# One three-level store instead of two half stores for a batch's last 64 output rows

## The chip, the cores and the metric

One core of one Trainium2 chip runs the kernel. The metric is the device time of one execution in microseconds (us); lower is better. It is quoted as the median of 3 runs. Beside it stands one profiled execution, with its own time, its span (from the first to the last instruction of the program) and its trace.

## The reference

Three stages follow each other on 4 batches of 576 rows: an attention over 8 heads with two sparse masks, a mixture of 4 causal attention experts with a top-2 gate, and a gated convolution block. All is float32 at the interface. Cut to what matters here, the last stage is:

```
x  = sparse_attention(q, k, v)            # [4, 576, 512]
x  = mixture_of_experts(x, ...)           # [4, 576, 512]
h  = max(x @ w_in, 0)                     # [4, 576, 1024]
c  = conv over 3 rows of h, one weight per channel
out = (h * sigmoid(c)) @ w_out            # [4, 576, 512]
```

The store of `out` is what changes. A batch has 576 = 4 x 128 + 64 output rows of 512 floats.

## The kernel before, in words

Every part of the work is a Python generator (a unit) of a kind: L loads, S the sparse attention, W weights, V, Q and A the experts' attention, M the gate of the last block, N its output product. A long string `ORDER` names, two characters at a time, which unit takes its next step. That string is the order in which each engine gets its instructions. It is the same before and after.

The units that matter here are `m_out` (batches 0 to 2, one unit per output tile) and `m_last` (batch 3, all five tiles in one unit). Both end in `m_put`, which copies an output tile from PSUM to an SBUF tile `ob` on ScalarE (ACT, through the helper at line 139) and then stores it with a DMA issued by SyncE (SP). `ob` has two buffers, which are used in turn.

Tiles t = 0 to 3 are 128 rows of 512 floats and are stored by one DMA at L733. Tile t = 4 has only 64 rows. Its product is computed in two halves of 256 columns, side by side in the partitions (L707): columns 0 to 255 of the 64 rows stand in partitions 0 to 63, and columns 256 to 511 of the same rows in partitions 64 to 127. In the output the two halves of a row lie next to each other. Line 736 stores them with two DMAs, one for each half.

SP issues all loads and stores of this kernel but the loads of `w_out`, and the 80 DMA transposes of the attention weights (L629, from `pn` to `apt`), in one queue and in the order of `ORDER`. Each DMA takes the next of eight completion semaphores (DMAHW0 to DMAHW7) and waits for the DMA that used it eight DMAs earlier. At the end of the program (L939) SP waits for every one of these semaphores, and the engines meet at a barrier.

Of the kernel before, what the change touches and what calls it, by code (L numbers as in the profile page):

```python
# [95 lines left out]
def moe_stack_kernel(ctx, tc, qk_in, vloc, vstr, w_p, wo_t, w_in, conv_w, w_out, out):  # L96
    nc = tc.nc
    ctx.enter_context(tc.manual_schedule())
    B, S, _ = vstr.shape
# [38 lines left out]
    def copy_a(out, in_, scale=1.0):  # L138
        act.activation(out=out, in_=in_, func=ACTF.Copy, scale=scale)  # L139
# [547 lines left out]
    def m_out(b, t):  # L687
        ps = bank("o")
        q0 = 128 * t
        half = DM // 2  # L690
        ps = ps if t < NG else ps[:, 0:half]
        for f in range(KF):
            g = [x[:, f % 2, q0:min(q0 + 128, S)] for x in gT[b, f - f % 2]]
            m_mul(ps, t, g, f)
            if f % 2:
                yield
        yield from m_put(b, t, ps)
# [13 lines left out]
    def m_last(b):  # L711
        for k in range(KF // 2):
            if k == 0:
                pairs = [banks("oe") for _ in range(2)]
                ends.extend([p[:, n] for p in pairs for n in range(2)] + [bank("o")[:, 0:DM // 2]])
            for t in range(NT):
                q0 = 128 * t
                for f in (2 * k, 2 * k + 1):
                    m_mul(ends[t], t, [x[:, f % 2, q0:min(q0 + 128, S)] for x in gT[b, 2 * k]], f)
                yield  # L720
        for t in range(NT):
            yield from m_put(b, t, ends[t])
            if t < NT - 1:
                yield

    def m_put(b, t, ps):
        q0 = 128 * t
        half = DM // 2
        ob = late["g"].tile([128, DM], F32, tag="ob", bufs=2, name="ob")
        copy_a(ob[:, 0:ps.shape[1]], ps, 1.0 / (G_S * W_S))  # L730
        yield
        if t < NG:
            nc.sync.dma_start(out=out[b, q0:q0 + 128, :], in_=ob)  # L733
        else:
            for n in range(2):
                nc.sync.dma_start(out=out[b, q0:S, half * n:half * n + half], in_=ob[64 * n:64 * n + 64, 0:half])


    late = {"pf": pool("pf", PF_BUFS), "pt": pool("pt", PF_BUFS), "z": pool("z", Z_BUFS),
# [204 lines left out]
```

## Time and profile before

| what | value |
|---|---|
| median of 3 runs | 378.42 us (377.3 to 379.41) |
| the profiled execution | 378.94 us |
| its span | 377.2 us |
| TensorE (PE) busy | 341.3 us, 90% |
| mean granted TensorE clock | 0.986 of full speed |
| stores of 128 x 512 (L733) | 16 DMAs of 256 KB |
| half stores of 64 x 256 (L736) | 8 DMAs of 64 KB, two for each batch |

The span is 1.7 us shorter than the profiled execution's time; the rest lies around it. Of the four pairs of half stores, three are issued while other work goes on (from 213.6, 313.2 and 334.7 us) and one, from 373.4 us, is the last thing that the program does.

### The profile page before, as it was taken

What the parts mean: (1) busy time and instruction counts of PE and PEld (TensorE: products, weight loads), DVE (VectorE), ACT (ScalarE), POOL (GpSimd) and SP (SyncE); (2) the same over time, 40 slices, a digit from 0 to 9 for tenths busy, and PEclk for the clock granted to TensorE, in tenths of its full rate; (3) what the DMA queues carried; (4) which work ended last, traced back from release to release, by engine and by line L of the source; (5) the groups of instructions that cost most, each with busy time, mean ns of one, the idle gap of its engine ahead of it and who ended that gap; (6) DMA issues with size and microseconds to landing.
All of it is one profiled execution on the core that took longest, in us unless ns stands there. A gap on an engine that the chain in (4) does not pass through costs nothing.

```text
span 377.2 us, 12596 instructions
## 1 busy us (share of the span) xinstructions
PE 341.3 (90%) x5139; PEld 227.8 (60%) x5139; DVE 309.0 (82%) x729; ACT 278.8 (74%) x628; POOL 59.4 (16%) x194
## 2 busy tenths in 40 slices
PE   4167699999789999999999999999999999999995
PEld 3146466667557666777557577776555576564542
DVE  6889879999969999999988758999998858693520
ACT  2468657878878998988887589997895796753522
POOL 8533430111400003000031005001000030000000
PEclk9999989999969999999999999999999999999999
DMA  7997968555867971893025724244536574010003
GB/s 269 285 271 221 285 221 235 164 167 124 119 86 122 181 123 30 195 162 69 3 58 127 121 58 106 47 79 85 100 76 120 79 134 90 20 53 28 3 26 127
DMA packets 79210, 45.94 MB, mean 122 GB/s; under 512 B 63792, under 2 KB 72496, under 8 KB 79152
## 3 DMA queue, kind: packets, MB, share of 16 engines
q1 hardware_dynamic: 78000, 40.94, 50.3%
q0 software_dynamic: 1152, 4.19, 3.5%
q8 instruction: 40, 0.66, 0.7%
q14 instruction: 18, 0.15, 0.1%
HBM read 25.20 MB, written 4.72 MB: 79 GB/s over the span
## 4 chain that ended last, share of the span: by engine, by line
PE 52%; ACT 17%; DVE 13%; DMA 13%; issue 4%; SPq 1%; POOL 0%; ACTq 0%; POOLq 0%; DVEq 0%
PE o L704 14%; DMA apt<-pn 7%; PE oe L704 6%; PE zav L638 4%; PE hps L145 4%; PE hps L146 3%; PE hps L147 3%; ACT pn L139 3%; PE o L707 2%; DMA vn<-in_dram 2%; PE psq L145 2%; DMA st<-in_dram 2%; PE psq L146 2%; PE psq L147 2%; ACT apf L602 2%
## 5 line engine op out<-in xcount | busy, mean ns | idle before, releaser
L704 PE MATMUL o<-wout,hs 128*128 128x512 f16 x288 | 66.2, 379 | 0.0
L704 PEld LDWEIGHTS <-hs 128*128 128x128 f16 x384 | 36.6, 98 | 41.9 <-issue 1.6
L673 DVE SCALAR_TENSOR_TENSOR t<-hs,taps,t 128x576 f32<-128x576 f32 x64 | 48.7, 809 | 6.4 <-ACT t L139 6.4
L139 ACT ACTIVATE pn<-apf,aden 64x64 f16<-64x64 f32 (+4 forms) x80 | 42.4, 557 | 9.2 <-DVE aden L611 2.8
L625 DVE SCALAR_TENSOR_TENSOR pn<-apf,aden,pn 128x320 f16<-128x320 f32 (+4 forms) x80 | 42.2, 544 | 6.1 <-ACT pn L139 5.4
L145 PE MATMUL psq<-xt,wqk 128*128 128x288 f16 x128 | 37.9, 296 | 1.0 <-DVE anm L593 0.7
L145 PE MATMUL hps<-z,wp 128*128 128x288 f16 x128 | 36.7, 287 | 1.6 <-ACT hs L665 1.0
L146 PE MATMUL psq<-xt,wqk 128*128 128x288 f16 x128 | 37.7, 295 | 0.0
L147 PE MATMUL psq<-xt,wqk 128*128 128x288 f16 x128 | 37.7, 295 | 0.0
L147 PE MATMUL hps<-z,wp 128*128 128x288 f16 x128 | 36.6, 286 | 0.0
L146 PE MATMUL hps<-z,wp 128*128 128x288 f16 x128 | 36.6, 286 | 0.0
L602 ACT ACTIVATE apf<-asc,anm 64x64 f32<-64x64 f32 (+3 forms) x64 | 29.7, 468 | 5.3 <-DVE anm L587 3.5
L620 POOL MEMSET pn<- 128x64 uint32 (+1 forms) x80 | 10.8, 153 | 130.6 <-DMA apt<-pn 80.0
L638 PE MATMUL zav<-apt,v 128*64 128x128 f16 (+1 forms) x720 | 27.4, 220 | 3.4 <-DMA apt<-pn 2.0
L638 PEld LDWEIGHTS <-v 128*64 128x64 f16 x720 | 22.1, 110 | 11.9 <-issue 10.9
L665 ACT ACTIVATE hs<-hps 128x576 f32<-128x576 f32 x32 | 20.6, 648 | 11.1 <-PE hps L147 6.4
L679 DVE SCALAR_TENSOR_TENSOR t<-t,hs 128x1152 f32<-128x1152 f32 x16 | 21.4, 1351 | 6.5 <-ACT t L677 6.5
L677 ACT ACTIVATE t<-t 128x1152 f32<-128x1152 f32 x16 | 18.6, 1162 | 9.1 <-DVE t L673 9.1
L136 POOL COPY bn<-lp 32x320 f32<-32x320 f32 x31 | 16.8, 543 | 51.7 <-PE av L377 32.5
L586 DVE TENSOR_REDUCE anm<-asc 64x2 f32<-64x128 f32 (+3 forms) x32 | 21.6, 674 | 2.7 <-PE asc L578 2.7
L139 ACT ACTIVATE t<-hs,taps 128x576 f32<-128x576 f32 x32 | 23.5, 770 | 0.1
L139 ACT ACTIVATE qk<-psq 128x576 f16<-128x576 f32 x32 | 20.3, 647 | 2.9 <-PE psq L147 2.0
(183 smaller groups left out, 812.3 us busy)
## 6 DMA issues: line engine op xcount, KB each, us to landing
st<-in_dram SPq DMA_DIRECT2D x9, 512.0 KB
ow<-in_dram POOLq DMA_DIRECT2D x8, 512.0 KB, 9.4
out_dram<-ob SPq DMA_DIRECT2D x16, 256.0 KB
ul<-in_dram SPq DMA_DIRECT2D x12, 288.0 KB
ul<-in_dram SPq DMA_DIRECT2D x12, 252.0 KB
vs<-in_dram SPq DMA_DIRECT2D x16, 144.0 KB
vn<-in_dram SPq DMA_DIRECT2D x8, 256.0 KB
st<-in_dram SPq DMA_DIRECT2D x4, 386.0 KB
```

The lines of the kernel that those rows point to most:

```text
L139: act.activation(out=out, in_=in_, func=ACTF.Copy, scale=scale)
L145: nc.tensor.matmul(out=out, lhsT=ah, rhs=bh, start=first, stop=False)
L146: nc.tensor.matmul(out=out, lhsT=al, rhs=bh, start=False, stop=False)
L147: nc.tensor.matmul(out=out, lhsT=ah, rhs=bl, start=False, stop=last)
L586: dve.tensor_reduce(out=nm[:, 0], in_=asc[:rows, :, :w], axis=mybir.AxisListType.X, op=ALU.max)
L602: act.activation(out=pfs[par], in_=scs[par], func=ACTF.Exp, scale=C2, bias=nm[:, 0, par:par + 1], accum_out=den[:, par:par + 1])
L625: dve.scalar_tensor_tensor(out=pn[:, 1, :w], in0=pfs[par], scalar=den[:, par:par + 1], in1=pn[:, 0, :w], op0=ALU.mult, op1=ALU.subtract)
L638: nc.tensor.matmul(out=av[64 * par:64 * par + 64, 0:rows], lhsT=v2[a][:, kb, D * e:D * e + D], rhs=pts[par][:, l, kb], start=(kb == 0 and ...
L665: act.activation(out=hs[:, i, 1:S + 1].rearrange("p (a n) -> p a n", a=2), in_=ps, func=ACTF.Relu, scale=1.0 / W_S)
L673: dve.scalar_tensor_tensor(out=t_[:, i], in0=tap, scalar=w, in1=t_[:, i], op0=ALU.mult, op1=ALU.add)
L679: dve.scalar_tensor_tensor(out=t_, in0=t_, scalar=1.0, in1=hs[:, :, 1:S + 1], op0=ALU.add, op1=ALU.mult)
L704: nc.tensor.matmul(out=ps, lhsT=g[a], rhs=wout[l][:, f], **at)
```

## The change

The two DMAs become one. Its DRAM side is written as a pattern of three levels: 2 halves, 64 rows, 256 floats. Its SBUF side is the whole tile: 128 partitions of 256 floats. The bytes and where they land are the same.

```
         else:
-            for n in range(2):
-                nc.sync.dma_start(out=out[b, q0:S, half * n:half * n + half], in_=ob[64 * n:64 * n + 64, 0:half])
+            nc.sync.dma_start(out=out[b, q0:S].rearrange("p (n c) -> n p c", n=2), in_=ob[:, 0:half])
```

On the other engines the instructions and their order are unchanged. On SP one instruction goes in each batch. Before, in SP's queue, around batch 0's last tile (`apt<-pn` is a transpose, `out_dram<-ob` a store, the shape is that of the DMA's destination):

```order
L629 DMA_TRANSPOSE apt<-pn_176 128x2x64 [waits DVE_49,DMAHW1_49,PE_49,Pool_49]
L736 DMA out_dram<-ob 64x256
L736 DMA out_dram<-ob 64x256 [waits DMAHW7_49]
L629 DMA_TRANSPOSE apt<-pn_174 128x2x64 [waits DVE_49,DMAHW0_49,PE_49,DMAHW2_49,Activation_49,Pool_49]
L629 DMA_TRANSPOSE apt<-pn_175 128x2x64 [waits DMAHW3_49,PE_49]
```

And after, in the same place:

```order
L629 DMA_TRANSPOSE apt<-pn_176 128x2x64 [waits DVE_49,DMAHW1_49,PE_49,Pool_49]
L735 DMA out_dram<-ob 2x64x256
L629 DMA_TRANSPOSE apt<-pn_174 128x2x64 [waits DVE_49,DMAHW2_49,PE_49,DMAHW7_49,Activation_49,Pool_49]
L629 DMA_TRANSPOSE apt<-pn_175 128x2x64 [waits DMAHW3_49,DMAHW0_49,PE_49]
```

One store stands where two stood, and each later DMA takes a semaphore that is one lower in the round. The end of SP's queue before, with the last stores of batch 3:

```order
L733 DMA out_dram<-ob 128x512 [waits DMAHW6_49,Activation_49]
L733 DMA out_dram<-ob 128x512 [waits DMAHW7_49,Activation_49]
L736 DMA out_dram<-ob 64x256 [waits DMAHW0_49,Activation_49]
L736 DMA out_dram<-ob 64x256 [waits DMAHW1_49]
L939 UNCONDITIONAL_BRANCH
```

And after:

```order
L733 DMA out_dram<-ob 128x512 [waits DMAHW3_49,Activation_49]
L733 DMA out_dram<-ob 128x512 [waits DMAHW4_49,Activation_49]
L735 DMA out_dram<-ob 2x64x256 [waits DMAHW5_49,Activation_49]
L938 UNCONDITIONAL_BRANCH
```

The last store was the one on DMAHW1, and is now on DMAHW5, four DMAs having gone in all.

## Rows read from the trace of the kernel before

**Rows 1.** The profile's page: span, and the chain that ended last, by engine.

```profile
span 377.2 us, 12596 instructions
...
PE 52%; ACT 17%; DVE 13%; DMA 13%; issue 4%; SPq 1%; POOL 0%; ACTq 0%; POOLq 0%; DVEq 0%
```

**Rows 2.** Chain of waits, 366 to 378 us: start, length, what.

```profile
368.22 3.88 PE o L704 x18
372.11 0.80 PE o L707 x12
372.90 0.03 ACTq L139
372.93 0.04 issue
372.98 0.39 ACT ob L139
```

**Rows 3.** Timeline of SP's queue, 364 to 378 us: start, length, what.

```profile
366.29 6.86 SPq L733 DMA_DIRECT2D out_dram<-ob  x5
373.39 1.12 SPq L736 DMA_DIRECT2D out_dram<-ob  x2
```

**Rows 4.** Stores' issues on SP: ns min/median/max, first and last start.

```profile
L733 SPq DMA_DIRECT2D out_dram<-ob x16: 332/342/585, 193.8 to 372.8; - x16
L736 SPq DMA_DIRECT2D out_dram<-ob x8: 472/588/591, 213.6 to 373.9; - x8
```

**Rows 5.** Stretches of the end: engines' busy time, PE clock, DMA share, GB/s.

```profile
373.70:374.10 0.40, 0.00 (x0) 0.00 (x0) 0.00 (x0) 0.00 (x0) 0.00 (x0) 1.00 1.01 394
374.50:375.10 0.60, 0.00 (x0) 0.00 (x0) 0.00 (x0) 0.00 (x0) 0.00 (x0) 1.00 0.45 109
375.10:375.70 0.60, 0.00 (x0) 0.00 (x0) 0.00 (x0) 0.00 (x0) 0.00 (x0) 1.00 0.44 109
375.70:376.00 0.30, 0.00 (x0) 0.00 (x0) 0.00 (x0) 0.00 (x0) 0.00 (x0) 1.00 0.00 0
```

**Rows 6.** SP's own L939 instructions, 375.95 to 376.5 us; SP's waits from 374.

```profile
L939 SPq EVENT_SEMAPHORE  x7: 28/28/28, 376.0 to 376.4; - x7
L939 SPq DRAIN  x2: 7/7/7, 376.4 to 376.5; - x2
...
SPq L939 <- DMA out_dram<-ob: 1.3, 2, 0.8
```

**Rows 7.** Loads of 18 x 8 x 256 (L321): SP's timeline, then stretches as in rows 5.

```profile
93.70 0.88 SPq L321 DMA_DIRECT2D vs<-in_dram  x2
...
168.41 3.65 SPq L321 DMA_DIRECT2D vs<-in_dram  x3
...
95.40:95.60 0.20, 0.20 (x12) 0.20 (x6) 0.20 (x2) 0.20 (x1) 0.20 (x1) 1.00 0.51 179
95.60:95.80 0.20, 0.20 (x12) 0.16 (x8) 0.17 (x2) 0.20 (x1) 0.20 (x1) 1.00 0.53 189
172.20:172.40 0.20, 0.20 (x4) 0.17 (x2) 0.20 (x2) 0.20 (x1) 0.00 (x0) 1.00 0.57 205
```

**Rows 8.** SP's timeline around the half stores of batches 0, 1 and 2.

```profile
213.61 1.22 SPq L736 DMA_DIRECT2D out_dram<-ob  x2
215.94 8.62 SPq L629 DMA_TRANSPOSE apt<-pn  x5
...
313.18 1.22 SPq L736 DMA_DIRECT2D out_dram<-ob  x2
328.76 2.35 SPq L733 DMA_DIRECT2D out_dram<-ob  x2
334.66 1.11 SPq L736 DMA_DIRECT2D out_dram<-ob  x2
345.63 0.34 SPq L733 DMA_DIRECT2D out_dram<-ob  x1
```

**Rows 9.** Batch 0: two stretches as in rows 5, then the timelines of POOL, ACT, DVE.

```profile
214.70:216.00 1.30, 0.47 (x16) 0.50 (x17) 0.96 (x6) 0.68 (x4) 0.16 (x1) 1.00 0.41 101
216.90:217.50 0.60, 0.60 (x7) 0.48 (x6) 0.60 (x3) 0.60 (x4) 0.00 (x0) 1.00 0.24 55
...
218.33 0.15 POOL L620 MEMSET pn<- 128x64 uint32 x1 [3.40 <-DMA apt<-pn]
...
218.85 0.45 ACT L139 ACTIVATE pn<-apf,aden 128x192 f16<-128x192 f32 x1
...
219.41 0.42 DVE L625 SCALAR_TENSOR_TENSOR pn<-apf,aden,pn 128x192 f16<-128x192 f32 x1 [0.72 <-ACT pn L139]
...
221.39 1.19 SPq L629 DMA_TRANSPOSE apt<-pn  x1
```

## The prediction

> **What bounds the kernel now.** I began with the page. Over the whole span the chain that ended last is half TensorE, and the DMA part of it is 13% [rows 1]; but a change of one store can only matter where a store is waited for, so the page's averages say little here. Next I read the chain's last pieces. The reader is to see that TensorE's last product ends at about 372.9 us and ACT's last copy at 373.4 us [rows 2]. That leaves 377.2 - 373.4 = 3.8 us in which no engine computes. Then I read SP's timeline for the same stretch: the last pair of half stores is issued from 373.39 to 374.51 [rows 3]. What follows is bound by DMA alone, and the stretches show it: the first half's data moves between 374.5 and 375.1, the second's between 375.1 and 375.7, at 109 GB/s in each (109 x 0.6 = 65 KB, one half of 64 KB), and after 375.7 nothing moves [rows 5]. SP sees the last landing at 376.0, and the waits for the other queues, the drain and the barrier take the rest [rows 6].
>
> So this end has a price that counts in full, about 2.2 us from the first byte to the last landing's being seen and 0.7 of issue, while the other three pairs lie in the middle of the kernel, where they count only if someone waits for them.
>
> **The change part by part.**
>
> *The issue.* One issue goes. The half stores take 472 to 591 ns each on SP [rows 4], so 0.6 us of SP's time is saved per batch. In the last batch the second half's data could not start before its own issue; in the other three SP's next instruction starts later anyway: at 215.94 after an end at 214.83, at 328.76 after 314.40, at 345.63 after 335.77 [rows 8]. I take nothing for those three. In the new store the first byte moves where the first half's moved before, at 374.5, 1.1 us after the issue began at 373.39; if its issue is one of the long ones (591 against 472), 0.1 later.
>
> *How many DMA engines carry it.* This is the term that decides. 128 packets of 1 KB have to move in either case. If all 16 engines share them, that is 8 each. The trace has a transfer that shows how the sharing goes: the loads of L321 write 18 x 8 x 256 floats, 144 packets of 1 KB, which 16 engines could share as 9 each. Where two or three such loads are queued and little else moves, the DMA share is 0.51 to 0.57 [rows 7], while a store of 128 rows reaches 1.01 [rows 5]. 9 of 16 engines is 0.56, and 9 is the largest divisor of 18 that is not over 16. So these engines are dealt by the outermost count of the pattern and not by the number of packets. The new store's DRAM side begins with a count of 2; its SBUF side with 128. If the smaller decides, 2 engines move 64 packets each. No transfer in this trace has sides that begin with different counts, so I bound the term from both sides: 16 engines as for the 128-row stores, or 2. The value I take is 2, because the outermost count is what the nearest row follows and a split into more than 2 would have to cut inside the DRAM side's first level.
>
> The Trainium skill, "DMA: Bandwidth & Descriptors", in "Why a DMA increments its semaphore by 16 and not by 1", says that the number of engines is the largest number up to 16 that divides the slowest dimension of both sides; by it 18 rows give 9, as the trace has it, and the new store 2, which is the forecast below. The same page, in "Rules for kernel authors", advises against two transfers to disjoint partition halves and for one transfer of 128 partitions; by that sentence alone the change would gain, which is the first rival.
>
> *The price of a packet.* In the two stretches of the loads 189 and 205 GB/s over 9 engines are 21.0 and 22.8 GB/s each, or 49 and 45 ns for 1024 bytes [rows 7]. The half stores themselves are dearer: 0.45 x 16 x 0.6 us / 64 = 67 ns for a packet [rows 5]; but there 16 engines read 64 partitions at once. The 128-row store moves 394 / (1.01 x 16) = 24.4 GB/s per engine, 42 ns for each KB [rows 5]. Two engines alone should not crowd each other, so I take 48 ns, the middle of the loads' two figures and a little, and keep 42 and 67 as the ends: 64 x 48 = 3.1 us, from 2.7 to 4.3.
>
> *The sum at the end.* Data moved from 374.5 to 375.65, 1.1 us (the stretch to 375.7 holds all of it). Now it takes 3.1 us from the same start: +2.0. Against that, SP's final waits. After the last landing it still had seven semaphore waits and a drain to go through, from 376.0 to 376.4 [rows 6], 0.06 us each. The last store was on DMAHW1 and is now on DMAHW5. If SP goes through the queues by number, four of these waits are done before the landing: -0.24 (an estimate from that row, as the row does not name the queues). Landing, barrier and ACT's copy before are as they were. Sum: +1.75 us, 378.94 + 1.75 = 380.7 for an execution like the profiled one, with 1.7 us around the span. The profiled execution is 0.5 above the median of the runs, so the forecast for the median is 378.42 + 1.75 = 380.2 us.
>
> *The stores in the middle.* The store of batch 0 would keep two engines until 214.7 + 3.1 = 217.8, where both halves were done by 216.0 [rows 9]. SP issues the next transposes from 215.94, and their data moves in 216.9 to 217.5 [rows 9]; on two engines it would queue behind the store, so that the first transpose lands 0.4 to 0.9 us later. Behind it wait POOL's memset at 218.33, which had waited 3.40 us for a transpose, and ACT's copy to the same `pn` at 218.85; after them DVE's step at 219.41, and only at 221.39 the transpose that uses it [rows 9]. Between DVE's end at 219.83 and that transpose lie 1.5 us. I cost this at nothing; what hides it is TensorE's work, for which this transpose waits in any case. With 67 ns packets the store would hold the engines to 219.0, the first transpose would be 1.5 to 2 us late, ACT's queue would stand still, and up to 0.7 could come through. After batches 1 and 2 SP issues nothing for 14 and 10 us, so a store of 3 to 4 us delays nobody.
>
> **The rivals.**
>
> *All 16 engines (faster).* The new transfer is dealt by the SBUF side's 128 partitions. For it: every 128-row store is, and both halves were. Against it: rows 7. Then 128 x 67 / 16 = 0.54 us of data from 374.5, ending at 375.1 instead of 375.65, and -0.24: -0.8 us, 377.6.
>
> *Two engines with dear packets, and a delay that comes through (slower beyond 0.5%).* Place: the last store, and the transposes behind batch 0's. Price: 64 x 67 = 4.3 us, +3.2 - 0.24 = +2.9 at the end, and 0 to 0.7 at batch 0: 381.4 to 382.0. It decides from 51 ns per packet on, where the end alone passes +1.9. For it: the only 1 KB stores in this trace take 67. Against it: these had 16 engines on 64 partitions, and the 2 KB stores take 42 per KB with all engines busy.
>
> *Hidden anyway.* If the end of the program waited for something else by then, the store's length would not show. The stretches after 373.5 show no engine busy [rows 5], so I give this next to nothing.
>
> **How the numbers follow.** Two engines at 42 to 50 ns: 70%, +1.4 to +2.2 us. All 16: 12%. Dear packets or a delay in the middle: 16%. The rest 2%. The runs before lie within 377.3 to 379.41, so a median of three can be 0.7 us off by itself; the forecast's own range is 379.1 to 381.3. For 8 in 10 I reach down to 378.3, which leaves out most of the 16-engine case, and up to 381.9. The bound of 0.5%, about what a measurement of this kernel can tell from no change, is 1.9 us, and my +1.75 stands just below it. Of the 70%, I give 28 to slower and 42 to within the bound; the 16-engine case is within it (10) or faster (2), the dear packets nearly all slower. Together: slower 0.44, within 0.53, faster 0.03.
>
> **What would show it.** In the changed kernel the stretch after the last issue should show a DMA share near 2/16 = 0.12 at about 42 GB/s for some 3 us, and SP's L938 waits should end near 378 with two left after the landing. After 214.7 the same low share should stand for 3 us, and the step at 221.39 should not move against its neighbours. A share near 0.45 for 0.6 us would mean that all 16 engines took part and that my reading of the outermost count is wrong; 0.12 for over 4 us, that the price of a packet was.

## The result and the profile after

The changed kernel takes 384.43 us (median of 6 runs, 383.07 to 386.35); the kernel before, measured beside it, 379.26 us (6 runs, 377.3 to 379.95). The ratio is 1.0149 (95% interval [1.011, 1.0187]): slower by 1.5%, and the medians lie 5.2 us apart, outside the range of the prediction, which ended at 381.9. Measured twice more (below), the same change came out at 1.0065 [1.0031, 1.0098] and 1.0056 [1.0022, 1.0089], by these ratios 2.1 to 2.5 us. So there are two questions: what costs 2 us each time, and what the other 3 us of the first measurement were. Medians here are of all runs, while ratios leave out slow ones (over 1.5% above the fastest of the same kernel), of which the profiled run of `e8_two_queues` is one.

The profiled execution of the changed kernel took 383.23 us, with a span of 381.5 against 377.2 [rows 1]. I read it from the back. First the last pieces of the chain of waits (start, length, what), which answer to [rows 2]:

```profile
370.27 3.88 PE o L704 x18
374.15 0.80 PE o L707 x12
374.95 0.03 ACTq L139
374.98 0.04 issue
375.02 0.38 ACT ob L139
```

The pieces and their lengths are those of before, 2.04 us later. ACT ends at 375.41, so 381.54 - 375.41 = 6.13 us of end are left, where before had 3.87 (the unrounded spans are 377.23 and 381.54). Of the 4.3 us by which the span grew, 2.26 lie behind the last copy and 2.04 ahead of it.

SP's timeline (start, length, what) shows the one issue in place of two [rows 3], and the lines below it its length in ns (min/median/max) beside the 128-row stores' [rows 4]:

```profile
371.73 3.46 SPq L733 DMA_DIRECT2D out_dram<-ob  x2
375.61 0.52 SPq L735 DMA_DIRECT2D out_dram<-ob  x1
...
L733 SPq DMA_DIRECT2D out_dram<-ob x16: 332/342/581, 195.4 to 374.9; - x16
L735 SPq DMA_DIRECT2D out_dram<-ob x4: 517/540/639, 216.0 to 375.6; - x4
```

Then the stretches of the end (length, busy time of PE, PEld, DVE, ACT and POOL, PE clock, DMA share, GB/s), which answer to [rows 5]:

```profile
375.70:376.30 0.60, 0.00 (x0) 0.00 (x0) 0.00 (x0) 0.00 (x0) 0.00 (x0) 1.00 0.99 386
...
376.70:377.70 1.00, 0.00 (x0) 0.00 (x0) 0.00 (x0) 0.00 (x0) 0.00 (x0) 1.00 0.12 33
377.70:378.70 1.00, 0.00 (x0) 0.00 (x0) 0.00 (x0) 0.00 (x0) 0.00 (x0) 1.00 0.13 30
378.70:379.70 1.00, 0.00 (x0) 0.00 (x0) 0.00 (x0) 0.00 (x0) 0.00 (x0) 0.76 0.14 48
379.70:380.20 0.50, 0.00 (x0) 0.00 (x0) 0.00 (x0) 0.00 (x0) 0.00 (x0) 0.50 0.12 41
380.20:380.60 0.40, 0.00 (x0) 0.00 (x0) 0.00 (x0) 0.00 (x0) 0.00 (x0) 0.50 0.00 0
```

The reader is to see the share: 0.99 while a 128-row store runs, and then 0.12 to 0.14 for some three and a half microseconds, 2/16 = 0.125, at 30 to 48 GB/s. Before it was 0.45 at 109 GB/s for 1.2 us. The granted clock falls to 0.50 (1.2 GHz) here, after TensorE's last product at 374.95, so it slows no work. In the same stretch cut finer (40 slices of 0.175 us from 375), the flow isn't even:

```profile
GB/s 0 0 0 0 386 398 374 304 82 0 35 12 47 47 47 23 23 41 35 18 18 53 47 47 47 47 47 53 47 18 0 0 0 0 0 0 0 0 0 0
```

47 GB/s is 8 packets in a slice, 4 on each engine: 44 ns for one packet. In the slices at 18 and 23 half of them or more are missing. Packet by packet in the trace, the data runs from 376.77 to 380.16 us, 3.39 us for 64 packets on each engine, 53 ns apiece. The packets that take long, 16 to 18 of the 128 and up to 267 ns each, stand at nearly the same places of the store in all three profiles of the change, and the last of them begins 1.95 us after the first byte. The 60 or so behind it follow each other at 42.3 ns on each engine, the price of the 128-row store. Why the first part stalls was not tried.

Behind the landing SP has fewer waits left [rows 6]:

```profile
L938 SPq EVENT_SEMAPHORE  x4: 17/28/28, 380.5 to 380.9; - x4
L938 SPq DRAIN  x2: 7/10/13, 380.7 to 380.8; - x2
...
SPq L938 <- DMA out_dram<-ob: 4.0, 2, 3.5
```

Of the four semaphore instructions the first, at 380.51, is the wait that sees the landing, two more follow, and the one at 380.9 already belongs to the barrier behind the drains. Before, six followed the one that saw the landing. The 3.5 us is the wait for the new store; before, the longest of these waits was 0.8 us [rows 6].

Last, batch 0, where the middle could have paid: SP, a stretch of the store's data (a DMA share of 0.13 here too), ACT, POOL and DVE in the changed kernel, which answer to [rows 8, 9]:

```profile
215.95 0.64 SPq L735 DMA_DIRECT2D out_dram<-ob  x1
217.73 1.19 SPq L629 DMA_TRANSPOSE apt<-pn  x1
...
217.20:218.70 1.50, 1.50 (x34) 1.24 (x34) 1.40 (x7) 0.86 (x4) 0.07 (x1) 1.00 0.13 33
...
221.28 0.45 ACT L139 ACTIVATE pn<-apf,aden 128x192 f16<-128x192 f32 x1 [0.53 <-DMA apt<-pn]
221.37 0.15 POOL L620 MEMSET pn<- 128x64 uint32 x1 [4.09 <-DMA apt<-pn]
221.85 0.42 DVE L625 SCALAR_TENSOR_TENSOR pn<-apf,aden,pn 128x192 f16<-128x192 f32 x1 [1.37 <-ACT pn L139]
223.18 1.19 SPq L629 DMA_TRANSPOSE apt<-pn  x1
```

Counted from the first transpose's issue (215.94 before, 217.73 after), POOL's memset comes at 3.64 instead of 2.39, ACT's copy at 3.55 instead of 2.91, and the next transpose at 5.45 both times. The delay is there, 1.25 us of it, and it is used up ahead of the step at which it could have been passed on.

### The profile page after: what moved, and what is told of

The parts are those of the page before. It is cut to its first block, busy times and chain, and to the rows that moved or that the text cites. A ratio compares the mean times of both kernels' runs of the same rounds, so it can differ in the third digit from the quotient of the medians.

```text
span 381.5 us, 12591 instructions
## 1 busy us (share of the span) xinstructions
PE 342.3 (90%) x5139; PEld 228.7 (60%) x5139; DVE 309.1 (81%) x729; ACT 278.7 (73%) x628; POOL 59.3 (16%) x194
## 4 chain that ended last, share of the span: by engine, by line
PE 53%; ACT 16%; DVE 13%; DMA 12%; issue 4%; SPq 1%; POOL 0%; ACTq 0%; POOLq 0%; DVEq 0%
PE o L704 14%; DMA apt<-pn 6%; PE oe L704 5%; DMA vn<-in_dram 5%; PE zav L638 4%; PE hps L145 4%; PE hps L146 3%; PE hps L147 3%; PE o L707 3%; ACT pn L139 3%; PE av L377 3%; ACT xt L139 2%; PE psq L145 2%; PE asc L578 2%; PE psq L146 2%
```

## The experiments

**The theory**: the last store's data goes through two engines, since its DRAM side begins with a count of 2; that lengthens the end by about 2.2 us each time, and the middle stores cost nothing. The rest of the first measurement is scatter that lies ahead of the change's first instruction. **The rivals**: the middle stores (or something that the change does to the whole program) cost the other 3 us; or the end is long for another reason than the number of engines, such as the pattern's third level.

### The same kernel again, and the change again

No edit: `e1_same_again` is the kernel before under a new label, `e2_change_again` the changed one.

> The kernel before, unchanged, as a second copy. It says how far two copies of one program lie apart. Every theory that puts the cost into the stores expects 1.000 (0.995 to 1.005), and a start of the first 30 us like that of the profile before, within 0.3 us. The rival that much of the 5 us is scatter of the start-up loads between programs expects it to differ by up to 1.1 us already at 30 us.

> The change, a second time. Stores alone: +2.2 us at the end (from ACT's last copy to the end of the span 6.1 us against 3.9), nothing before 213 us. If the rest of the 5 us belongs to the change, the ratio is again 1.011 to 1.019 and the rest shows somewhere between 213 and 375 us. If it is scatter between programs, the ratio can fall to 1.006 and the start differs from the first profile of the changed kernel, where 1.1 us had been lost by 30 us.

Measured: the copy 379.42 us against 379.04 (35 runs of before, 375.65 to 382.8), ratio 1.0026 [0.9994, 1.0058]; the change 381.42 us, 1.0065 [1.0031, 1.0098]. In the profile of the second the end is 6.12 us long and its stretches are those of above:

```profile
372.82 0.39 ACT L139 ACTIVATE ob<-o 128x256 f32<-128x256 f32 x1 [0.18 <-PE o L707]
...
374.40:375.40 1.00, 0.00 (x0) 0.00 (x0) 0.00 (x0) 0.00 (x0) 0.00 (x0) 0.84 0.13 40
375.40:376.40 1.00, 0.00 (x0) 0.00 (x0) 0.00 (x0) 0.00 (x0) 0.00 (x0) 0.50 0.13 27
376.40:377.40 1.00, 0.00 (x0) 0.00 (x0) 0.00 (x0) 0.00 (x0) 0.00 (x0) 0.50 0.13 47
```

ACT's last copy ends at 373.21, 0.16 us earlier than before, and the span is 379.3: a long end behind a body that is not longer. So the end's 2.25 us come back and the rest does not. The copy's start missed what was expected: the step that TensorE had reached at 30 us in the profile of before comes 3.2 us later in the copy, where 0.3 was expected and 1.1 by the rival, and yet the spans are 377.2 and 377.5. So two copies of one program can be 3 us apart in their start.

### Only the last store, only the first three

```
e3_last_only:                              e4_first_three:
+ if b == 3:                               + if b < 3:
+     one store, "p (n c) -> n p c"        +     one store, "p (n c) -> n p c"
+ else:                                    + else:
+     two half stores                      +     two half stores
```

> One three-level store in batch 3 alone; batches 0 to 2 keep their two half stores. Theory (two engines at the end): +2.2 us plus up to 0.24 since the last store stays on the first queue's semaphore, a ratio of 1.006. Rival (the store of batch 0 delays the transposes behind it, and this makes the other 3 us): the same +2.2 here, the rest in the next kernel. Rival (all is scatter): cannot be told from 1.000 to 1.015.

> One three-level store in batches 0 to 2; batch 3 keeps two half stores. Theory (only the end pays): 0 to +0.3 us, a ratio of 1.000. Rival (batch 0's store delays the transposes behind it, and TensorE with them): +3 us, 1.008, with the loss between 213 and 230 us in the trace.

Measured: the last store alone 382.45 us, 1.0099 [1.0066, 1.0132]; the first three alone 378.77 us, 0.9987 [0.9949, 1.0026]. Their ends are 6.31 and 3.82 us long. Two rows of the stretches of `e3_last_only` and one of SP's timeline of `e4_first_three` suffice:

```profile
376.50:377.50 1.00, 0.00 (x0) 0.00 (x0) 0.00 (x0) 0.00 (x0) 0.00 (x0) 1.00 0.14 36
377.50:378.50 1.00, 0.00 (x0) 0.00 (x0) 0.00 (x0) 0.00 (x0) 0.00 (x0) 0.67 0.13 32
```

```profile
374.56 1.17 SPq L739 DMA_DIRECT2D out_dram<-ob  x2
```

The loss is in the last store. That it alone is dearer than the whole change in its second and third measurement is within what one such ratio is off: their intervals overlap. One piece of it can be read: in `e3_last_only` the last store takes the completion semaphore DMAHW0, as fewer DMAs were issued before it, and then SP's waits behind the landing are not saved; its end is 0.18 us longer than that of the whole change, though its issue begins 0.03 us after ACT's end and not 0.21. The middle stores cost nothing that is measured; by the interval, 1.0 us is the most.

### The outermost count: 4, 8 and 16

```
- for n in range(2):
-     nc.sync.dma_start(out=out[b, q0:S, half * n:half * n + half], in_=ob[64 * n:64 * n + 64, 0:half])
+ rows = out[b, q0:S].rearrange("p (n c) -> (p n) c", n=2)
+ nc.sync.dma_start(out=rows.rearrange("(a s) c -> s a c", s=4), in_=ob[:, 0:half])   # s = 4, 8, 16
```

The same 128 packets of 1 KB go to the same 64 rows in one store, also with three levels, but the DRAM side begins with 4, 8 or 16. The rows land in another order than they have to, so these kernels are for measuring alone.

> One three-level store in every batch as in the change, with the same 128 packets of 1 KB to the same 64 KB blocks, but the DRAM side's levels are 4, 32, 256 instead of 2, 64, 256; so the tail's rows land permuted within the tail. Theory (the outermost count sets the number of engines): 4 engines, 32 packets each at the 53 ns of the change, 1.7 us of data at a DMA share of 0.25, and 4.4 us from ACT's last copy to the end of the span (the change 6.1, before 3.9). Rival (any three-level store runs on 2 engines): 3.4 us of data at 0.12, 6.1 us.

> The same with levels 8, 16, 256 (rows of the tail permuted). Theory: 8 engines, 16 packets each, 0.85 us of data at a share of 0.5, 3.5 us from ACT's last copy to the end. Rival (2 engines for any three-level store): 6.1 us.

> The same with levels 16, 8, 256 (rows of the tail permuted). Theory: 16 engines, 8 packets each, 0.45 to 0.6 us of data, 3.1 us from ACT's last copy to the end, 0.8 us less than before, a ratio of 0.998 (0.995 to 1.001): one transfer is then better than two. Rival (2 engines for any three-level store): ratio 1.006 to 1.010 as the change.

Measured: one execution each of 4 and 8, at 381.76 and 380.24 us; 16 at 379.67 us against 378.47 (23 runs of before, 377.1 to 385.28), ratio 1.0024 [0.9993, 1.0055]. What tells is the stretches, from `e5_outer4`, `e6_outer8` and `e7_outer16`:

```profile
376.50:377.40 0.90, 0.00 (x0) 0.00 (x0) 0.00 (x0) 0.00 (x0) 0.00 (x0) 1.00 0.17 33
377.40:378.30 0.90, 0.00 (x0) 0.00 (x0) 0.00 (x0) 0.00 (x0) 0.00 (x0) 1.00 0.27 91
```

```profile
375.90:376.40 0.50, 0.00 (x0) 0.00 (x0) 0.00 (x0) 0.00 (x0) 0.00 (x0) 1.00 0.29 51
376.40:376.90 0.50, 0.00 (x0) 0.00 (x0) 0.00 (x0) 0.00 (x0) 0.00 (x0) 1.00 0.46 143
```

```profile
377.70:378.10 0.40, 0.00 (x0) 0.00 (x0) 0.00 (x0) 0.00 (x0) 0.00 (x0) 1.00 0.75 218
```

In the later stretch of each the share is near 4/16 and 8/16, and three quarters of all with 16, where the store is too short to fill a stretch; the earlier stretches begin ahead of the data. The traces also have packets of 4 bytes behind the data, and their numbers are 16 behind each half store and 2, 4, 8 and 16 behind the stores of the series. Read packet by packet, all in us, the end counted from ACT's last copy to the last instruction:

| outermost count | data of the last store | end |
|---|---|---|
| two half stores (before) | 1.09 | 3.87 |
| 2 (the change) | 3.39 | 6.13 |
| 4 | 1.82 | 4.59 |
| 8 | 1.03 | 3.88 |
| 16 | 0.73 | 3.52 |

So the third level is not the price, and one store in place of two isn't either: with a first count of 8 the end equals that of the two halves, with 16 it is 0.35 us shorter. In the whole time that gain isn't seen (1.0024, where 0.998 was expected), and the three ends are 0.2 to 0.4 us longer than expected. The count decides. The Trainium skill, "DMA: Bandwidth & Descriptors", in "Why a DMA increments its semaphore by 16 and not by 1", says this of the slowest dimension of both sides, and all four counts agree; in its "Rules for kernel authors" the advice to use one transfer of 128 partitions in place of two on partition halves does not hold for this DRAM side, 6.13 us against 3.87.

### Two queues for the last two halves

```
+ eng = nc.scalar if n and b == 3 else nc.sync
+ eng.dma_start(out=out[b, q0:S, half * n:half * n + half], in_=ob[64 * n:64 * n + 64, 0:half])
```

This asks the end from the other side: the two half stores stay, and the second one's issue no longer waits for the first's.

> Two half stores in every batch as before, but batch 3's second half is issued by ACT, which is idle by then, beside the first on SP. Theory (each half runs on 16 engines and the second waits only for its issue): both halves' data move together from the same time, 0.6 to 0.8 us in all, 3.4 us from ACT's last copy to the end instead of 3.9, a ratio of 0.999. Rival (ACT's first DMA of the kernel is slow to start): 3.9 us or more, 1.000 to 1.003.

Measured: 379.86 us, 1.0022 [0.9986, 1.0057]. The two issues stand beside each other, on SP and on ACT's queue, and the data of both moves together:

```profile
377.96 0.48 SPq L737 DMA_DIRECT2D out_dram<-ob  x1
...
377.97 0.56 ACTq L737 DMA_DIRECT2D out_dram<-ob  x1
...
379.20:379.80 0.60, 0.00 (x0) 0.00 (x0) 0.00 (x0) 0.00 (x0) 0.00 (x0) 1.00 0.77 195
```

The data takes 0.73 us and the end 3.59, which is 0.28 less than before (3.4 was expected). That is under 0.1% of the time and is not seen in the ratio. What the two ways tried here, this one and the count of 16, win on this end is therefore about 0.3 us, and what the change loses about 2.3.

### The change and the kernel before a third time

No edit: the other 3 us of the first measurement were still open, and so both ran once more, beside each other.

> The change a third time, since its two measurements, 1.0149 and 1.0065, lie further apart than their intervals. Theory (the end costs 2.25 us, as every profile so far shows, and the rest is scatter of the loads at the start): a ratio of 1.006, and again 6.1 us from ACT's last copy to the end of the span. Rival (the change costs 5 us, and the second measurement was low): 1.011 or more, with a loss in the trace beside the end's 2.25 that starts after 213 us.

> The kernel before, unchanged, beside it. Both theories: 1.000, within 0.003; 3.87 us from ACT's last copy to the end. A start of the first 30 us that differs from the first profile by 1 us or more would show once more what scatter alone does.

Measured: the change 380.92 us against 379.31 (23 runs of before, 375.95 to 382.45), 1.0056 [1.0022, 1.0089]; the copy 378.61 us, 0.9985 [0.9952, 1.0019]. The end of the change is 6.13 us long again, that of the copy 3.87. Where executions differ ahead of the change is seen from the first 128-row store, which is issued before any changed instruction. Its row, whose first time is that start, in the copy, then in the change the second and third time; before and the first profile of the change have 193.8 [rows 4] and 195.4:

```profile
L733 SPq DMA_DIRECT2D out_dram<-ob x16: 332/342/584, 192.9 to 371.2; - x16
```

```profile
L733 SPq DMA_DIRECT2D out_dram<-ob x16: 332/338/587, 192.6 to 372.7; - x16
```

```profile
L733 SPq DMA_DIRECT2D out_dram<-ob x16: 332/342/582, 195.8 to 375.0; - x16
```

Over eleven profiles (without `e8_two_queues`) that start lies between 192.6 (a run of the change) and 196.5 (`e7_outer16`), while from there to the last 128-row store it is 178.3 to 180.2 us in every kernel. So some 4 us of scatter are there before the kernels differ in anything that has run. It begins early: between 16 and 20 us of the span TensorE (the first of the five busy times) did 0.89 us of work in before's profile and 0.07 in that of the change, with the DMA engines full in both:

```profile
16.00:20.00 4.00, 0.89 (x89) 0.85 (x89) 2.98 (x7) 2.36 (x5) 3.31 (x6) 1.00 1.08 276
```

```profile
16.00:20.00 4.00, 0.07 (x11) 0.07 (x17) 2.75 (x6) 1.70 (x4) 3.31 (x6) 1.00 1.10 251
```

A second place lies between 100 and 120 us, here in before's profile and in that of its copy `e1_same_again`:

```profile
100.00:120.00 20.00, 16.34 (x303) 10.78 (x301) 16.44 (x53) 15.64 (x43) 3.19 (x15) 0.83 0.67 101
```

```profile
100.00:120.00 20.00, 16.02 (x333) 11.57 (x331) 18.43 (x58) 17.52 (x51) 4.90 (x18) 1.00 0.66 106
```

The granted clock (the third number from the end) is 0.83 in the first and 1.00 in the second, as part of this stretch ran at 1.2 instead of 2.4 GHz in the first; the copy, which was 2.4 us behind at 100 us, is level with it at 120.

## Why the prediction was wrong, point by point

**Right: what the end waits for.** The path is TensorE's last product, ACT's copy, the store, SP's last waits, and nothing took its place; the longer store is seen in the end with nothing to hide it.

**Right: two engines.** The share is 0.12 to 0.14 as said, and the series 2, 4, 8, 16 shows that the outermost count deals them. The 16-engine rival is out.

**Right: the final waits, -0.24.** Two semaphore waits were left after the landing as the prediction said (the seven that it counted before are the one that sees the landing and six behind it), and `e3_last_only`, whose store has another semaphore, ended 0.18 us later in spite of an earlier issue.

**Right: the middle costs nothing.** POOL's step came 1.25 us later, and the transpose at 221.39 kept its place against its neighbours (5.45 us both times). I had expected the first transpose up to 0.9 us late. By the interval of `e4_first_three`, 1.0 us is the most that the middle can cost.

**A size off: the end.** Forecast +1.75, measured +2.26 (6.13 less 3.87). Two terms make the difference. The data was 64 x 48 = 3.1 us in the sum and is 3.39: 42 ns a packet where nothing stalls, as in the 128-row stores, and some 0.6 us of stalls, 53 ns on the mean. And the sum let the issue begin where it began before; it began 0.18 us later behind ACT's end, so the first byte moved 1.37 us after that end instead of 1.17. 0.3 + 0.2 are the 0.5 us. That 53 is past the 51 ns from which, as the prediction said, the change's end passes 0.5%, so on the price of a packet its rival of dear packets decides, if only just, and none of that rival's delay in the middle came through; the two later ratios, 1.0065 and 1.0056, are just past 0.5%.

**Two figures that don't follow from its rows.** From the first byte at 374.5 to the landing's being seen at 376.0 are 1.5 us, not 2.2; the sum doesn't use it. And packets of 50 ns give 3.2 - 1.1 - 0.24 = +1.9 us, not the +2.2 at the upper end of the 70%, which is 55 ns.

**The failed step: the scatter in the range.** "A median of three can be 0.7 us off by itself" was read from three runs that happened to lie within 2.1 us. The 81 runs of before made since lie between 375.65 and 385.28, and of threes drawn from them at random 2 in 10 have a median over 1.4 us off. With twice that scatter and the end at +2.26 the range would have had to reach about 383 (381.9 + 0.7 + 0.5).

**Still open.** Even so it would not have held 384.43, which is 6.0 us above the 378.42 that the forecast started from. Of these 0.8 are that start, as six runs of before beside the change have 379.26, and 2.26 are the end; 2.9 are not explained. In the profiled execution, 383.23 us, 2.04 were lost ahead of the last copy, 1.64 of them before 200 us (TensorE's offset against before), ahead of the first changed instruction at 215.95. But six runs of six were above 383.06, where of the 24 later runs of the change only six are, so plain chance between executions doesn't explain the first six. Nor does the change, by its two later measurements. The later runs were on three chips (0, 10 and 8), on which before took 379.04, 378.47 and 379.31 us; the chip of the first six is not on record. Their mean granted clocks are low, 0.977 to 0.984. Of the 22 later runs of the change that count for its ratios, the seven in this range have a median of 382.7 us and the other fifteen 380.4, so a lower clock goes with a longer time. Whether it is the cause in the first six isn't shown, as only one of them has a trace. What they had in common isn't settled.

## What to carry to other kernels

Before two transfers are made one, write down what stands outermost on each side: a leading 2 on one side leaves two engines, however many packets there are, and with 8 or 16 in its place (and the rows in another order) the same bytes in one store were even with the halves or 0.35 us better at the end. Here the transfer behind the last computation counted in full, and the same transfer in the middle, about 3.4 us of data against 1.1 to 2.0 before, cost nothing that was measured. And read the scatter of a kernel from more than three runs before a range rests on it.

## What was not expected of the hardware

- Two engines alone do not move 1 KB packets evenly: 42.3 ns each in the last 1.4 us, and single packets of up to 267 ns in the first 2 us, at nearly the same places in all three profiles of the change; 53 ns on the mean (3.39 us for 64).
- In the changed kernel, and in those with 4, 8 and 16, the last store's issue begins 0.2 us after ACT's end and not 0.03 as before. In `e3_last_only`, with the same store on another semaphore, it is 0.03 again; in `e4_first_three`, with half stores last, 0.21. So it goes with the semaphore (DMAHW5 against DMAHW0) and not with the store's shape; why was not tried.
- The time from the first instruction to the first output store differs by some 4 us between executions (192.6 to 196.5 us), though the kernels are the same up to there.
